# The input's own accumulate issued ahead of the base, operands begun in three slots of four, and the last block's first half in h's banks

## The chip, the cores and the metric

One core of a Trainium2 chip runs the whole program. The metric is device time in microseconds (us), the median of several executions. Engines are named as the profile names them: PE (TensorE), DVE (VectorE), ACT (ScalarE), POOL (GpSimd), SP (SyncE); PEld is PE's weight load.

## What is computed

2048 tokens of 512 features are normalised; the result is the input plus a state-space convolution of the normalised rows plus a mixture of eight experts, all eight of which every token uses:

```python
x = A_u
xn = _layernorm(x, axis=-1)
return x + _A_ref(xn, ...) + _B_ref(xn, ...)

# in _A_ref: K from dt, A, B, C (512 features, 128 states), then a causal convolution by FFT, and
y = ... + u * Dskip[None, None, :]

# in _B_ref, with K = E = 8, D = 512, F = 1792:
for e in range(E):
    mask = (topk_idx == e)
    w = (gates * mask).sum(-1, keepdims=True)
    h = _silu(xf @ w1[e]) @ w2[e]
    out = out + w * h
```

## The kernel before

**Blocks and slots.** The experts' work runs over 32 blocks: expert `e` (0 to 7) outside, quarter of the tokens `tb` (0 to 3, 512 tokens each) inside. A block runs over four steps `d` (three with two pairs of feature groups, the last with one), each step over four slots `s`. Seven products take the place of eight (Strassen's scheme), each in three fp16 parts. A step computes products of `w1` and `xop` into three PSUM banks, `hb`; ACT copies partial sums out of them (`scC`, `sE`, `scB`) or copies one bank into another (`hb<-hb`), and two DMAs that POOL issues add `sE` into `scC` (in slot 2) and into `scB` (in slot 3). ACT takes the summed `scC` up (L1584) at the start of the next step.

**The side of w2.** Before block (6,2), a unit is a product `y` of `ahl` and `w2s` (L1551 to L1553). From (6,2) on (`seven`), this side uses seven products too: `prep` brings a step's four quarters into operands `pl` and `st` in three stages (`prep_sums` on DVE, `prep_high` on ACT, `prep_low` on DVE), `pops2` gives PE units of 21 matmuls (L1783) on four banks `z`, once operands are ready, and `reads` takes a finished half (`th`, 1 ahead of 0) out of these banks. The last half of the last block uses the banks of `hb` and one more.

**What sums up the result.** `oacc[i]`, one DRAM tile for each 128 tokens, collects it. Expert 0 writes `ye` there (L1531), later experts add theirs by accumulating DMAs on POOL's queue (L1529); the four `ye` of a block are issued in the next block. In blocks (1,1), (1,2), (2,1) and (2,2), `base(i)` loads normalised rows, `base_add(i)` scales them by `Dskip` on DVE, and `base_send(i)` adds them into `oacc[i]` (L1512), then adds the input's rows `u` from DRAM (L1514). The convolution's result `ys4` is added at the end (L2010). For the first eight `i`, `oacc` is then copied to `out` (L2012); the last four are loaded back, combined in SBUF and sent in halves.

**What sets the order.** The program is written out in one order for each engine: `slot` calls the pieces of a slot in turn, `put(key, f)` hangs a piece on a slot, and a planner with estimated costs (`clock`, `room_now`) decides which conversions of weights go into a slot. Each engine issues its own instructions in that order, DMAs included, and a wait holds what is behind it on its queue. Two DMAs that accumulate into the same `oacc[i]` are kept apart by a wait of the issuing queue for the first one's landing.

Of the kernel before, what the change touches and what calls it, by code (L numbers as in the profile page):

```python
# [14 lines left out]
ALU = mybir.AluOpType  # L15
# [3 lines left out]
P = 128  # L19
# [17 lines left out]
def s4_moe_kernel(  # L37
# [15 lines left out]
    nc = tc.nc  # L53
# [3 lines left out]
    NT = NTOK // P  # L57
    KT = D // P
    E, NPR = w1.shape[0], w1.shape[1]
    NF = 2 * NPR  # L60
    TB = 512
    NB = NTOK // TB
    TPB = TB // P
# [8 lines left out]
    BG0 = (0, 2, 1, 0)  # L72
    SW = (6, 2)
    ROOM = 0.0
    LAG = 3

    RING = 2
# [27 lines left out]
    oacc = [dr.tile([P, D], F32, name=f"oacc{i}") for i in range(NT)]  # L105
# [387 lines left out]
    rows = {}  # L493
# [607 lines left out]
    def now():  # L1101
        return clock["slot"]
# [205 lines left out]
    for pr in range(3, NPR):  # L1308
        for h in range(2):
            n = 2 * (pr - 3) + h  # L1310
# [170 lines left out]
    def room_now():  # L1481
        return min(clock["actleft"], 2.0) + clock["pe"] - clock["pe1"] - clock["act"] + clock["act0"]
# [27 lines left out]

    def base_send(i):
        nc.gpsimd.dma_start(oacc[i], stg[i], accum_op=ALU.add)  # L1512
        halves = [a.rearrange("p (h d) -> h p d", h=2) for a in (oacc[i], u[i * P:(i + 1) * P, :])]
        nc.gpsimd.dma_start(*halves, accum_op=ALU.add)  # L1514


    units = []
# [94 lines left out]
    pipe = {"step1": None, "step2": None, "began": 0, "ended": 0, "popped": False, "out": [], 0: 0, 1: 0, "pool": 0}  # L1612
# [37 lines left out]
    def place():  # L1650
        if pipe["pool"] < RING:
            return "pool"
        if live["n"] > NRAW - 2 or any(h > m for h, m in zip(held_q, (10, 2, 2))) or any(it.load and it.raw is None and it.ready() for it in work[:6]):
            return None
        return "raw"
# [57 lines left out]
        for q, pr in enumerate(DQS[d]):  # L1713
            units2.append((k, q, pr, now()))

    def prep():


        for n in (2, 1):
            if pipe[f"step{n}"] and (n == 2 or place() and (ready2() == 0 or room_now() > 0.5)):  # L1720
                if n == 1:
                    reserve(pipe["step1"][0])
                x, pipe[f"step{n}"] = pipe[f"step{n}"], None
                (prep_high, prep_low)[n - 1](x)
                if n == 1:
                    pipe["step2"] = x
        if order and not pipe["step1"] and now() > pipe["began"] + (len(open_) > 1 and len(order) < 6):
            k = order[0]
            if all((*k, f) in quarters and quarters[(*k, f)][1] < now() for f in range(2)):
                order.pop(0)  # L1730
                pipe["began"] = now()
                pipe["step1"] = prep_sums(k)
# [5 lines left out]
    def ready2():  # L1738
        n = 0
        for k, q, pr, at in units2:  # L1740
            if at >= now() or not w2_made(k[0], pr):
                break
            n += 1
        return n
# [15 lines left out]
    def pop2():  # L1760
        (e, tb, th, d), q, pr, _ = units2.pop(0)
        key = (e, tb, th, 2)
        c = count.get(key, 0)
        last = e == E - 1 and tb == NB - 1
        todo = [(open_[e, tb, th, d], q, pr)]
        if last and th == 0 and d > 1:
            while units2:
                k, q1, pr1, _ = units2.pop(0)
                todo.append((open_[k], q1, pr1))
        count[key] = c + len(todo)  # L1770
        if c == 0 and last and th == 0:
            take_bank()
            ys[key] = [*hb, ps_s.tile([P, 2, TH], F32, tag="s4", name="z3")]
        elif c == 0:
            ys[key] = [ps_y.tile([P, 2, TH], F32, tag=f"y{n}", name=f"z{e}_{tb}_{th}_{n}") for n in range(4)]
        began = set()
        for b, h, fa, ia, fb, ib in SEQ:
            for m, ((pl, st), q1, pr1) in enumerate(todo):
                wx, ws = x2["w"][pr1], w2s[pr1].rearrange("p a f (h c) -> p a (f h) c", h=2)
                rhs = ws[:, :, (0, 2, 3)[ib], :] if not fb else wx[:, :, ib - 1, :] if ib else ws[:, :, 1, :]  # L1780
                for n, (x, y) in enumerate(((0, 0), (0, 1), (1, 0))):
                    lhs = st[:, x, ia, q1, :] if fa else pl[:, x, q1, ia, :]
                    T.matmul(ys[key][b][:, h], lhs, rhs[:, y, :], start=(c == 0 and b not in began and m + n == 0),  # L1783
                             stop=(count[key] == NPR and m + 1 == len(todo) and n == 2), skip_group_check=True)
                began.add(b)
        clock["pe"] += 2.3 * len(todo)
        if q == len(DQS[d]) - 1:
            del open_[e, tb, th, d]
            release((e, tb, th, d))
            if th == 0:  # L1790
                done.add((e, tb, "y", d))
        if count[key] == NPR:
            pipe["ended"] = now()
            pipe["out"].append(lambda: (read_last if last else read)(e, tb, th, ys.pop(key)))
# [47 lines left out]
    def reads():  # L1842
        if "send" in pipe and pipe["send"][0] < now():
            pipe.pop("send")[1]()
        while pipe["out"]:
            pipe["out"].pop(0)()
# [12 lines left out]
    def put(key, f):  # L1859
        side.setdefault(key, []).append(f)  # L1860
# [45 lines left out]
    for tb in range(NB):  # L1906
        for j in range(TPB):
            i = tb * TPB + j
            eb = (1 + tb // 2, 1 + tb % 2)
            for n, f in ((7, base), (8 + j % 2, base_add), (11, base_send)):  # L1910
                n += 3 if j > 1 else 0
                n += 1 if j > 1 and f is base_send else 0
                put((*eb, n // 4, n % 4), lambda i=i, f=f: f(i))
        if tb:
            put((0, tb, 2, 0), lambda tb=tb: gates_mm(tb))
            put((0, tb, 2, 1), lambda tb=tb: gates_dve(tb))
# [11 lines left out]
    halves = [(g, a) for g in (2, 3) for a in range(2)]  # L1928
# [34 lines left out]
    def slot(e, tb, d, s, pops):  # L1963
        if "s4" in done and not x2 and (True, (SW[0], "w2", NPR - 1)) in made:
            second_open()
        for key in [key for key in late if key in done]:
            work[0:0] = late.pop(key)
        for f in mid.get((e, tb, d, s), ()):
            f()
        clock["conv"] = clock["read"] = 0  # L1970
        if e + tb == 0:
            work_lows()
        if seven(e, tb):
            if units:
                pop(min((2, 2, 1, 0)[s], len(units)))
            else:
                pops2(s)
        else:
            pop(pops)
        flush()  # L1980
        if seven(e, tb):
            prep()
        if e == 0:
            work_lows()
        room = clock["room"] = act_room()
        if room > 1.0 and run_later():
            room = min(room - 1.6, 1.0 if s in (1, 2) else room)
        for f in side.get((e, tb, d, s), ()):
            f()
        work_lows()  # L1990
        if e + tb and (d, s) == (len(DQS) - 1, 1):
            held.append(room)
        elif e + tb == 0 or tb == NB - 1:
            work_on(2 if e + tb == 0 or room > 2 and (e or d < 3) else 1)
        elif e == 0 and tb == 1:
            work_on(2 if (d, s) < (2, 1) else 1 if (d, s) == (2, 1) else 0)
        elif seven(e, tb):
            work_on(2 if room > (1.0 if e > SW[0] else 2.2) else 1 if room > -1.0 else 0)
        elif room > 1.0:
            work_on(1 if room < 2.2 or 0 < e and not x2 else 2)  # L2000
        if (e, tb, d, s) >= BG0:
            if (e, tb, d, s) == BG0:
                clock["pe"] = clock["pe0"] = clock["pe1"] = clock["dve"] = clock["dve0"] = 0.0
            bg_run()
        if seven(e, tb):
            reads()
        clock["slot"] += 1

    def s4_final(i):
        nc.gpsimd.dma_start(oacc[i], ys4[:, i, :], accum_op=ALU.add)  # L2010
        if i < NT - 2 * TPB:
            nc.sync.dma_start(out[i * P:(i + 1) * P, :], oacc[i])  # L2012

    for i in range(NT):
        put((E - 1, NB - 1 - (i >= NT // 2), i // 2 % 4, i % 2 * 3), lambda i=i: s4_final(i))

    def final_load(j):
        i = NT - TPB + j
# [145 lines left out]
    while units2 or order or pipe["step1"] or pipe["step2"]:  # L2164
        if units2 and pipe["out"] and units2[0][0][1:3] == (NB - 1, 1):
            reads()
        if units2 and units2[0][0] == (E - 1, NB - 1, 0, 2) and len(units2) < 3:
            pass
        else:
            pops2(None)  # L2170
        prep()
        if not order and not pipe["step1"] and not pipe["step2"]:
            reads()
        clock["slot"] += 1
# [57 lines left out]
```

## Time and profile before

| | us |
|---|---|
| median of three executions | 2514.57 (2514.34 to 2518.81) |
| the profiled execution | 2521.78 |
| its span on the core | 2519.7 |
| PE busy | 2313.6 |
| DVE busy | 1933.0 |
| ACT busy | 1522.8 |
| POOL busy | 373.8 |

In the profile, busy tenths show the span in 40 slices of 63 us; PEclk is the granted TensorE clock in tenths. In a list of waits, a row says which engine and line waited for which, us in total, times, and the longest. In a timeline a row has the start, the time from the first start to the last end, the engine and line, the operation and its tiles, and in brackets the idle time ahead of it with what ended it. A DMA's row gives its count, its KB and the median us from issue to landing.

### The profile page before, as it was taken

To read this page: it belongs to the slowest core of one execution; us is meant where nothing else is said; L and a number is where in the kernel's file an instruction comes from. 1 tells how busy PE (TensorE), PEld (TensorE's weight loads), DVE (VectorE), ACT (ScalarE), POOL (GpSimd) and SP (SyncE) were. 2 spreads that over 40 slices of the span, in tenths; PEclk is the share of its full clock that TensorE was granted. 3 is DMA by queue.
4 is the path that set the end of the run, shared out by engine and by line. 5 is a ranking of instruction groups with operands and counts; after the bars stand their busy time and mean duration, and the time that the engine had idled before them with its cause. 6 is when DMAs were issued, how large, how long until landed. Compare 5 with 4: busy or idle time off the path is not lost.

```text
span 2519.7 us, 48492 instructions
## 1 busy us (share of the span) xinstructions
PE 2313.6 (92%) x19033; PEld 1631.9 (65%) x19033; DVE 1933.0 (77%) x3868; ACT 1522.8 (60%) x2665; POOL 373.8 (15%) x411
## 2 busy tenths in 40 slices
PE   8999999575999493999999999999999999999996
PEld 4666666353666362666666666666666668878885
DVE  8868998574998383998999999999878343875556
ACT  7676766252666252666667666766656766766553
POOL 0000001111111111111111011111101111111220
PEclk9999999887999797999999999999999999999998
DMA  7686656453657462665555565566545666543662
GB/s 264 207 242 156 158 133 139 89 120 68 141 141 156 72 136 40 144 146 124 125 102 135 147 131 124 102 147 146 121 99 134 174 148 147 133 114 72 110 109 60
DMA packets 366357, 331.00 MB, mean 131 GB/s; under 512 B 216304, under 2 KB 256880, under 8 KB 365680
## 3 DMA queue, kind: packets, MB, share of 16 engines
q1 hardware_dynamic: 276656, 229.35, 31.4%
q0 software_dynamic: 88896, 98.03, 25.3%
q8 instruction: 149, 2.44, 0.4%
q14 instruction: 80, 0.66, 0.1%
q10 hardware_dynamic: 576, 0.52, 0.1%
HBM read 211.97 MB, written 70.25 MB: 112 GB/s over the span
## 4 chain that ended last, share of the span: by engine, by line
PE 73%; issue 10%; DMA 9%; DVE 3%; ACT 3%; POOL 2%; SPq 0%; DVEq 0%; POOLq 0%; ACTq 0%
PE hb L1568 33%; PE y L1552 10%; PE y L1553 10%; PE y L1551 10%; PE z L1783 5%; DMA scC<-sE 4%; DMA oacc<-base 1%; DMA scB<-sE 1%; PE kgen L922 1%; PE yp L1072 1%; PE uf L985 1%; PE kf L985 1%; POOL oacc L1512 1%; PE hb L2124 1%; DVE ahl L1597 0%
## 5 line engine op out<-in xcount | busy, mean ns | idle before, releaser
L1568 PE MATMUL hb<-xop,w1s 128*128 128x256 f16 x9114 | 1087.6, 275 | 134.9 <-ACT hb L2079 115.3
L1568 PEld LDWEIGHTS <-w1s 128*128 128x128 f16 x9114 | 891.9, 99 | 304.4 <-issue 137.5
L1552 PE MATMUL y<-w2s,ahl 128*128 128x512 f16 x1456 | 551.8, 379 | 0.9 <-DVE w2s L566 0.9
L1553 PE MATMUL y<-w2s,ahl 128*128 128x512 f16 x1456 | 551.8, 379 | 0.0
L1551 PE MATMUL y<-w2s,ahl 128*128 128x512 f16 x1456 | 551.8, 379 | 0.0
L2026 POOL DMA_DIRECT2D scC<-sE x117 | 114.6, 979 | 1152.1 <-ACT sE L2064 962.6
L1553 PEld LDWEIGHTS <-ahl 128*128 128x128 f16 x1456 | 142.5, 98 | 172.8 <-issue 1.2
L1552 PEld LDWEIGHTS <-ahl 128*128 128x128 f16 x1456 | 142.5, 98 | 130.5 <-issue 0.2
L1551 PEld LDWEIGHTS <-ahl 128*128 128x128 f16 x1456 | 142.5, 98 | 130.4
L1597 DVE SCALAR_TENSOR_TENSOR ahl<-scC,sc,ahl 128x512 f16<-128x512 f32 x100 | 67.9, 679 | 195.8 <-ACT ahl L1588 195.8
L1584 ACT ACTIVATE scC<-scC,sc 128x512 f32<-128x512 f32 (+1 forms) x97 | 64.8, 668 | 215.8 <-DMA scC<-sE 215.7
L1584 ACT ACTIVATE fa<-hb,sc 128x512 f32<-128x512 f32 (+1 forms) x204 | 129.6, 635 | 107.0 <-PE hb L1568 105.2
L1597 DVE SCALAR_TENSOR_TENSOR ahl<-fa,sc,ahl 128x512 f16<-128x512 f32 (+1 forms) x214 | 146.0, 683 | 50.7 <-ACT ahl L1588 50.2
L2026 POOL DMA_DIRECT2D scB<-sE x124 | 118.4, 955 | 394.4 <-ACT scB L2064 275.3
L2079 ACT COPY hb<-hb 128x512 f32<-128x512 f32 x124 | 64.4, 520 | 176.1 <-PE hb L1568 175.9
L1588 ACT ACTIVATE ahl<-fa,sc 128x512 f16<-128x512 f32 (+1 forms) x214 | 143.7, 672 | 8.6 <-DMA xnd<-xn 1.4
L908 DVE TENSOR_TENSOR tb<-tb,pt 128x64 f32<-128x64 f32 (+2 forms) x192 | 132.3, 689 | 6.6
L906 DVE TENSOR_TENSOR pt<-tb,zi 128x64 f32<-128x64 f32 (+2 forms) x192 | 131.5, 685 | 4.8
L1040 DVE TENSOR_TENSOR s<-s,tm 128x672 f32<-128x672 f32 (+6 forms) x224 | 127.8, 570 | 7.7
L2069 ACT COPY hb<-hb 128x512 f32<-128x512 f32 x124 | 64.9, 524 | 110.3 <-PE hb L1568 109.8
L907 DVE TENSOR_TENSOR tb<-tb,zr 128x64 f32<-128x64 f32 (+2 forms) x192 | 130.6, 680 | 0.0
L1039 DVE TENSOR_TENSOR tm<-v,k 128x672 f32<-128x672 f32 (+6 forms) x224 | 126.7, 566 | 4.6
(332 smaller groups left out, 3391.5 us busy)
## 6 DMA issues: line engine op xcount, KB each, us to landing
xop<-xd SPq DMA_DIRECT2D x210, 256.0 KB, 4.1
pp<-in_w_dram SPq DMA_DIRECT2D x98, 512.0 KB, 4.7
raw<-in_w_dram SPq DMA_DIRECT2D x56, 512.0 KB, 4.8
scB<-sE POOLq DMA_DIRECT2D x93, 256.0 KB, 4.1
scC<-sE POOLq DMA_DIRECT2D x89, 256.0 KB, 4.0
oacc<-ye POOLq DMA_DIRECT2D x88, 256.0 KB, 6.4
raw<-in_w_dram SPq DMA_DIRECT2D x52, 256.0 KB, 3.8
raw<-in_w_dram SPq DMA_DIRECT2D x104, 128.0 KB, 3.9
```

What stands on the lines that cost most here:

```text
L906: V.tensor_tensor(pt, tin[:, ::-1, r], ziv, op=ALU.mult)
L907: V.tensor_tensor(tout[:, :, r], tin[:, :, r], zrv, op=ALU.mult)
L908: V.tensor_tensor(tout[:, :, r], tout[:, :, r], pt, op=ALU.add)
L1040: V.tensor_tensor(s3[:, :, m:], s3[:, :, m:], tm, op=ALU.add)
L1551: T.matmul(y, lhs[0], w2s[pr][:, 0, fh, :], start=(c == 0), stop=False)
L1552: T.matmul(y, lhs[0], w2s[pr][:, 1, fh, :], start=False, stop=False)
L1553: T.matmul(y, lhs[1], w2s[pr][:, 0, fh, :], start=False, stop=(c == NF - 1))
L1568: T.matmul(dst[:, q, :], w1s[pr][:, a, wo, k * P:(k + 1) * P], xop[:, xo, b, k, :], start=(first_mm and q == 0 and n == 0), stop=(n == 5), ...
L1584: S.activation(fa, src[:, :n], AF.Silu, scale=w1_unscale(e, d if whole else prs[0]))
L1588: S.activation(ahl[:, 0, :n], fa, AF.Copy, scale=scales[e][:, 3:4])
L1597: V.scalar_tensor_tensor(ahl[:, 1, :n], fa, sc[:, 3:4], ahl[:, 0, :n], op0=ALU.mult, op1=ALU.subtract)
L2026: nc.gpsimd.dma_start(dst, src, accum_op=ALU.add)
```

## The change

There are five parts.

1. `base_send` no longer adds the input. A new `base_u(i)` does: the DMA's form is two times 64 rows of 512 elements (even and odd rows) where it was two times 128 rows of 256 (left and right halves), and it is put in slots 1 and 3 of steps 0 and 1.
2. `prep` gets the slot and begins `prep_high` only in slots 0 to 2, and only if the planner's `room_now` is over `RUSH` (0.0), also where no unit is ready. `reads` is called once more in a slot, right behind `prep`.
3. In these blocks one conversion of weights is allowed where `room` is over `TIGHT` (-0.3), before: over -1.0.
4. In the last block the first half (`th` = 1) goes to the banks of `hb` and the further bank, and the second half (`th` = 0) to the four banks `y`; before it was the other way round.
5. The copy of `oacc` to `out` is put in a slot of its own (`final_out`).

```diff
+    RUSH = 0.0
+    TIGHT = -0.3
...
     def base_send(i):
         nc.gpsimd.dma_start(oacc[i], stg[i], accum_op=ALU.add)
-        halves = [a.rearrange("p (h d) -> h p d", h=2) for a in (oacc[i], u[i * P:(i + 1) * P, :])]
-        nc.gpsimd.dma_start(*halves, accum_op=ALU.add)
+
+    def base_u(i):
+        rows = [a.rearrange("(b a) d -> a b d", a=2) for a in (oacc[i], u[i * P:(i + 1) * P, :])]
+        nc.gpsimd.dma_start(*rows, accum_op=ALU.add)
...
-    def prep():
+    def prep(s):
         for n in (2, 1):
-            if pipe[f"step{n}"] and (n == 2 or place() and (ready2() == 0 or room_now() > 0.5)):
+            if pipe[f"step{n}"] and (n == 2 or place() and s < 3 and room_now() > (0.5 if ready2() else RUSH)):
...
-        if c == 0 and last and th == 0:
+        if c == 0 and last and th == 1:
             take_bank()
             ys[key] = [*hb, ps_s.tile([P, 2, TH], F32, tag="s4", name="z3")]
...
             eb = (1 + tb // 2, 1 + tb % 2)
+            put((*eb, j // 2, 1 + j % 2 * 2), lambda i=i: base_u(i))
             for n, f in ((7, base), (8 + j % 2, base_add), (11, base_send)):
...
         if seven(e, tb):
-            prep()
+            prep(s)
+            if pipe["out"]:
+                reads()
...
-            work_on(2 if room > (1.0 if e > SW[0] else 2.2) else 1 if room > -1.0 else 0)
+            work_on(2 if room > (1.0 if e > SW[0] else 2.2) else 1 if room > TIGHT else 0)
...
     def s4_final(i):
         nc.gpsimd.dma_start(oacc[i], ys4[:, i, :], accum_op=ALU.add)
-        if i < NT - 2 * TPB:
-            nc.sync.dma_start(out[i * P:(i + 1) * P, :], oacc[i])
+
+    def final_out(i):
+        nc.sync.dma_start(out[i * P:(i + 1) * P, :], oacc[i])
 
     for i in range(NT):
         put((E - 1, NB - 1 - (i >= NT // 2), i // 2 % 4, i % 2 * 3), lambda i=i: s4_final(i))
+        if i < NT - 2 * TPB:
+            put((E - 1, NB - 1, min(i // 2 + i % 2, 3), (3, 1)[i % 2] + (i == NT // 2 - 1) * 2), lambda i=i: final_out(i))
...
-        prep()
+        prep(0)
```

Line numbers of the changed kernel are 4 to 10 higher than those of before. How the order on the engines moves is shown at two places. Up to block (6,2) only POOL's order differs; SP's is the same from end to end.

**POOL, block (1,1).** A name like `scC1_1_2` gives e, tb and d; `in_u_dram` is the input. Before, from the last adds of step 2 on:

```order
L2026 DMA scB1_1_2_5541<-sE1_1_2_5474 128x512
L1512 DMA oacc0_109<-base0_5279 128x512
L1514 DMA oacc0_109<-in_u_dram 2x128x256
L1512 DMA oacc1_110<-base1_5281 128x512
L1514 DMA oacc1_110<-in_u_dram 2x128x256
L2026 DMA scC1_1_3_5695<-sE1_1_3_5704 128x256
L2026 DMA scB1_1_3_5739<-sE1_1_3_5704 128x256
L1512 DMA oacc2_111<-base2_5491 128x512
L1514 DMA oacc2_111<-in_u_dram 2x128x256
L1512 DMA oacc3_112<-base3_5493 128x512
L1514 DMA oacc3_112<-in_u_dram 2x128x256
L2026 DMA scC1_2_0_5913<-sE1_2_0_5927 128x512
```

The four adds of the input are gone from there in the changed kernel, and stand in the first half of the block:

```order
L1518 DMA oacc0_109<-in_u_dram 2x64x512
L2036 DMA scC1_1_0_4913<-sE1_1_0_4927 128x512
L2036 DMA scB1_1_0_5036<-sE1_1_0_4927 128x512
L1518 DMA oacc1_110<-in_u_dram 2x64x512
L1533 DMA oacc2_111<-ye1_2_5129 128x512
L1533 DMA oacc3_112<-ye1_3_5132 128x512
L1533 DMA oacc0_109<-ye1_0_5141 128x512
L1533 DMA oacc1_110<-ye1_1_5144 128x512
L1518 DMA oacc2_111<-in_u_dram 2x64x512
L2036 DMA scC1_1_1_5195<-sE1_1_1_5209 128x512
L2036 DMA scB1_1_1_5265<-sE1_1_1_5209 128x512
L1518 DMA oacc3_112<-in_u_dram 2x64x512
```

The input's adds moved ahead of the base, two of them to either side of the four `ye`, which in this block add into the same `oacc`; `scC` of step 1 now stands right behind the third.

**ACT, block (7,1), between steps 2 and 3.** `pl` and `st` are the operands that `prep_high` writes, `o` the reading of a finished half, `hb1<-hb0` the copy with which step 3 begins. Before:

```order
L2064 COPY scB7_1_2_27045<-hb1_103 128x512
L1697 ACTIVATE pl7_0_0_1_27069<-q7_0_1_0_26011,sc7_23973 128x2x128
L1697 ACTIVATE pl7_0_0_1_27069<-scB7_0_1_26121,sc7_23973 128x2x256
L1697 ACTIVATE st7_0_0_1_27070<-sums7_0_0_1_26981,sc7_23973 128x1024
L1797 COPY o7_2_0_27079<-z7_0_1_0_26469 128x256
L2069 COPY hb1_103<-hb0_102 128x256
L1646 ACTIVATE scC7_1_2_26999<-scC7_1_2_26999,sc7_23973 128x512
```

And in the changed kernel:

```order
L2074 COPY scB7_1_2_27045<-hb1_103 128x512
L1801 COPY o7_2_0_27069<-z7_0_1_0_26469 128x256
L2079 COPY hb1_103<-hb0_102 128x256
L1650 ACTIVATE scC7_1_2_26999<-scC7_1_2_26999,sc7_23973 128x512
L1701 ACTIVATE pl7_0_0_1_27087<-q7_0_1_0_26011,sc7_23973 128x2x128
L1701 ACTIVATE pl7_0_0_1_27087<-scB7_0_1_26121,sc7_23973 128x2x256
L1701 ACTIVATE st7_0_0_1_27088<-sums7_0_0_1_26981,sc7_23973 128x1024
```

The three operand instructions moved from ahead of the bank copy to behind it and behind the take-up of `scC`. On PE, units that came in pairs at the start of a half come one at a time, a slot later.

## The prediction

> **What bounds the kernel now.** I read the page first, its slices above all, then the busy time block by block, then the waits, then the timeline at the places they name. (A block is one expert, e, on one quarter of the tokens, tb; four steps d, each of four slots s.)
>
> ```profile
> span 2519.7 us, 48492 instructions
> PE 2313.6 (92%) x19033; PEld 1631.9 (65%) x19033; DVE 1933.0 (77%) x3868; ACT 1522.8 (60%) x2665; POOL 373.8 (15%) x411
> PE   8999999575999493999999999999999999999996
> PEclk9999999887999797999999999999999999999998
> ```
>
> TensorE is the bound nearly everywhere; it has two holes, slices 7 to 9 and 13 to 15, and a short last slice. The holes by blocks (the stretches run from one block's first scC add to the next one's; columns: us, then PE, PEld, DVE, ACT, POOL busy, granted clock, DMA share, GB/s):
>
> ```profile
> 312.60:384.90 72.30, 72.30 (x577) 48.78 (x576) 67.74 (x122) 45.28 (x79) 6.91 (x9) 1.00 0.51 126
> 384.90:496.30 111.40, 89.95 (x805) 60.71 (x804) 81.58 (x172) 53.35 (x104) 21.46 (x21) 0.91 0.55 114
> 496.30:607.90 111.60, 76.91 (x650) 51.76 (x649) 72.31 (x155) 45.38 (x87) 22.19 (x22) 0.86 0.54 104
> 607.90:685.20 77.30, 61.49 (x419) 40.40 (x417) 57.36 (x96) 45.59 (x73) 11.43 (x13) 0.89 0.56 124
> 685.20:758.90 73.70, 73.51 (x641) 49.66 (x640) 69.27 (x142) 49.18 (x87) 10.58 (x12) 1.00 0.60 137
> 758.90:869.30 110.40, 89.45 (x754) 60.54 (x753) 73.97 (x147) 51.23 (x98) 21.22 (x20) 0.91 0.56 114
> 869.30:984.80 115.50, 78.13 (x653) 52.55 (x651) 70.16 (x148) 44.27 (x83) 22.25 (x21) 0.84 0.51 99
> 984.80:1064.70 79.90, 60.55 (x414) 39.92 (x413) 58.63 (x103) 46.39 (x77) 11.47 (x14) 0.87 0.55 122
> 1064.70:1139.40 74.70, 72.88 (x629) 49.04 (x628) 70.68 (x142) 48.76 (x87) 10.41 (x12) 1.00 0.58 134
> ```
>
> A block without base work takes 72.3, 73.7, 74.7: 73.6 in the mean. The six stretches that the four base blocks touch sum to 606.1, so the holes cost 606.1 - 6 x 73.6 = 164.5 us, PE's slower clock there included. Who is waited for in them (us in total, times, longest; all but the first row from windows over the holes):
>
> ```profile
> POOL oacc L1514 <- DMA oacc<-base: 175.8, 14, 18.6
> ACT scC L1584 <- DMA scC<-sE: 96.0, 6, 27.4
> ACT scC L1584 <- DMA scC<-sE: 101.7, 5, 27.7
> PE hb L1568 <- ACT hb L2079: 91.3, 6, 21.0
> PE yp L206 <- ACT k L1003: 35.6, 2, 18.0
> ```
>
> ACT waits 197.7 us in the two holes for the add of sE into scC, which POOL issues, and TensorE then waits for ACT's copies behind it. On POOL in block (1,1):
>
> ```profile
> 367.93 0.86 POOL L2026 DMA_DIRECT2D scB<-sE  x1 [1.80 <-ACT scB L2064]
> 391.22 0.86 POOL L2026 DMA_DIRECT2D scB<-sE  x1 [5.50 <-ACT scB L2064]
> 401.00 3.54 POOL L1529 DMA_DIRECT2D oacc<-ye  x4 [8.93 <-ACT ye L1525]
> 404.19 1.25 POOL L2026 DMA_DIRECT2D scC<-sE  x1
> 408.83 0.86 POOL L2026 DMA_DIRECT2D scB<-sE  x1 [3.39 <-ACT scB L2064]
> 457.23 1.96 POOL L1514 DMA_DIRECT2D oacc<-in_u_dram  x1 [18.57 <-DMA oacc<-base]
> 458.33 1.83 POOL L2026 DMA_DIRECT2D scC<-sE  x1
> 473.29 0.51 ACT L1584 ACTIVATE scC<-scC,sc 128x256 f32<-128x256 f32 x1 [27.40 <-DMA scC<-sE]
> ```
>
> POOL holds its queue until base has landed, then issues u, then the scC that stood behind it; ACT has it 473.29 - 458.33 = 15.0 after its issue and 16.1 after u's. So an add queued just behind u arrives with u.
>
> ```profile
> scC<-sE POOLq DMA_DIRECT2D x89, 256.0 KB, 4.0
> oacc<-ye POOLq DMA_DIRECT2D x88, 256.0 KB, 6.4
> oacc<-in_u_dram POOLq DMA_DIRECT2D x16, 256.0 KB, 15.8
> DMA to landing us min/median/max: 15.0/15.8/19.6
> ```
>
> The same 256 KB take 4.0 and 6.4 from SBUF, 15.8 from u (last row: u's line alone).
>
> **The change, part by part.** *u ahead of base (POOL).* What goes: 14 waits of u on base, and u's from the stretch between scC of steps 2 and 3 and the next block's first scC. With them go both ACT waits of each base block: -164.5. What comes: the same 16 u's, issued elsewhere. POOL issues as soon as its queue allows, so u0 goes out at once behind scB of the block before (367.93), 17 us ahead of this block's first scC (384.9): hidden, just, at 15.8. u1 goes out behind scB of step 0, at 391.22 + 0.86 = 392.1, lands 407.9. In (1,1) and (1,2) the four ye's add into the very rows of these u's: the last waits for u1 (natural 401.0 to 404.5, now 407.9), and u2 waits for the first ye, so it issues near 409. scC of step 1 (naturally 404.19) is right behind it and is used 16.1 after u2's issue, at 425.1. When would ACT want it? In block (2,0), without u:
>
> ```profile
> 705.60 0.86 POOL L2026 DMA_DIRECT2D scC<-sE  x1 [0.67 <-ACT sE L2064]
> 714.93 0.72 ACT L1584 ACTIVATE scC<-scC,sc 128x512 f32<-128x512 f32 x1 [0.74 <-DMA scC<-sE]
> ```
>
> ACT is there 714.19 - 705.60 = 8.6 after the issue: 412.8. So ACT waits 12.3. In (2,1) and (2,2) the ye's are other rows' and nothing waits: u2 issues at 404.5, scC is used at 420.6 if u1 and u2 run beside each other (wait 7.8), or 12.3 again if they run one after the other; I take 10, the middle, as no row shows which. u3 follows scB of step 1 and has 15 us until the (now later) scC of step 2: hidden. Base goes out where it did, waits for nothing new, and lands with the 6.4 of its like. Sum of ACT waits 2 x 12.3 + 2 x 10 = 44.6, against 197.7 before, which cost 164.5: at 0.83 per us, 37.
>
> The size of u's transfer is the one unknown: 64 rows of 512 elements in each of two parts in place of 128 rows of 256. Bounds from the rows: 6.4 (ye, same bytes, same destination) and 19.6 (slowest u). At 6.4 no add is late; at 19.6 u1 lands 411.7, u2 issues near 413, scC is used at 433, ACT waits 20 x 4, which is 66. I take 15.8, since source, destination, bytes and the count of two parts stay. The Trainium skill ("DMA: Bandwidth & Descriptors", Rules for kernel authors) says that an outermost dim of c < 16 confines a DMA to at most c engines; by that the new form is still on two engines, and u is no shorter. The trace's 15.8 against 6.4 for equal bytes agrees. The page adds (Why a DMA increments its semaphore by 16 and not by 1) that such small counts go to the next engines in turn; by that u1 and u2 would run beside each other, and the wait in (2,1) and (2,2) would be 7.8, some 4 us less in all. No row here shows it.
>
> *Cover that goes.* The holes hid DVE work: 81.58 + 72.31 + 57.36 = 211 us of DVE in three stretches that shrink from 300 to some 240, 88% busy. Other blocks run at 67.74 of 72.30 without a hole, so I charge 4 us in all (0 to 12).
>
> *prep in three of four slots, reads earlier, the two thresholds* (blocks from (6,2) on). PE's waits from 2060 us to the end:
>
> ```profile
> PE hb L1568 <- ACT hb L2069: 8.1, 5, 1.8
> PE hb L1568 <- ACT scC L2064: 7.3, 5, 2.4
> PE z L1783 <- DVE o L1798: 4.3, 2, 2.9
> PE hb L1568 <- ACT hb L2079: 3.3, 1, 3.3
> ```
>
> The five waits of the first row stand where the order of ACT shows three prep operations ahead of the hb copy; now they stand behind it: -8.1. On DVE and PE nothing is added, units come one at a time and a slot later. New waits of like size can appear behind the moved prep (the copy at L2079 is next): +2. Net -6; bounds -19 (all ACT waits of these rows go) and +8 (each moved one costs as much elsewhere).
>
> *Last block's first half in h's banks.* One stall at the end goes, where that half had to wait until the half before was read out of the y banks:
>
> ```profile
> 2465.69 0.49 PE L1783 MATMUL z<-w2s,pl 128*128 128x256 f16 x3 [2.87 <-DVE o L1798]
> 2467.46 0.80 PE L1783 MATMUL z<-w2s,st 128*128 128x256 f16 x3 [0.63 <-DVE o L1811]
> 2469.97 0.85 PE L1783 MATMUL z<-w2s,pl 128*128 128x256 f16 x3
> 2494.61 1.32 ACT L1818 ACTIVATE o<-o,gse 128x512 f32<-128x512 f32 x2
> ```
>
> 2.87 + 0.63, and some 2 us of triples at 0.85 in place of 0.49; but DVE works on the same operands at that time, so I take -3 (0 to -6). The closing chain stays as it is: the gate of block (7,2)'s last half (L1818) is still issued behind the last prep, and the final loads behind that.
>
> *final_out apart.* SP's order is the same row for row: 0.
>
> Sum: -164.5 + 37 + 4 - 6 - 3 = -132.5. The profiled execution took 2521.78 (span 2519.7), the median of the runs is 2514.57, 0.3% less; on the median 2514.57 - 132.5 = 2382.
>
> **The rivals.**
> - *No wait remains* (u lands in 6.4, or runs beside everything): -164.5 - 9 + 4, 2345. For it: the rows are twice as long and half as many. Against: 15.8 for the same bytes and the same two parts.
> - *The queue stays full*: u's run one after the other, u0 also delays scC of step 0 and u3 that of step 2. It needs only some 3 us more on each; ACT would wait some 25 to 30 in each base block, 83 to 100 us of cost in place of 37: 2430 to 2445. For it: the longest u took 19.6, and four u's of 15.8 are 63 of a block's 73.6 us.
> - *Slower than before*: u's form of longer rows costs more per byte. If they run one after the other, a base block can't be shorter than four of them: from 18.4 us a piece on the queue never empties and every add waits. The gain of 170 is used up where 4 u - 73.6 = 42, at 29 us for one u; at 32 us the blocks lose 4 x (128 - 73.6) = 218, and the time is 2514.57 - 164.5 + 218 + 4 - 9 = 2563. Nothing in the rows points to a price near that.
> - *The change doesn't do what it says*: u's new waits (ye on u, u on ye) hold POOL as base did. They exist in (1,1) and (1,2) alone, and are in the sum.
>
> **How the numbers follow.** A change under 0.2% (5 us) can't be told from none here. Chances: my forecast 0.62 (2355 to 2425), no wait 0.15, full queue 0.17, slower 0.04, within 0.2% 0.02. The forecast's range goes down to 2350 and up to 2430, which leaves out most of the first rival and of the second: 0.94 faster, 0.02 same, 0.04 slower.
>
> **What would show it.** The wait of POOL's u on base is gone; POOL waits some 4 us for u1 ahead of a ye in (1,1) and (1,2). ACT's waits for scC<-sE in the two stretches sum to about 45, all at step 1, 8 to 12 each; at steps 3 and 0 none is left. The base blocks take about 83 in place of 111, with the granted clock near 1. u lands in 14 to 17. The five waits on ACT hb at what is now L2079 are gone from (7,0) on, and at the last half's start PE waits under 1 us. Wrong would be: waits for scC at steps 0 or 2 (full queue), u under 10 or over 20, or a DVE that is over 95% busy in the base blocks with PE waiting for it.

## The result, and the profile after

The changed kernel takes 2402.24 us (median of 4 runs, 2398.95 to 2405.74) against 2516.14 for the kernel before on the same chip: a ratio of 0.9547, 95% interval 0.9529 to 0.9564. It is faster by 114 us. Forecast were 132.5 us less and 2382, range 2350 to 2430. The profiled execution took 2403.11 us with a span of 2401.3, so the trace shows 118.4 us less span than the one of before.

The head and the slices of its page, against those quoted of before:

```profile
span 2401.3 us, 48485 instructions
PE 2306.6 (96%) x19033; PEld 1627.8 (68%) x19033; DVE 1931.0 (80%) x3868; ACT 1523.4 (63%) x2665; POOL 365.2 (15%) x411
PE   8999999789998899999999999999999999999996
PEclk9999999899999999999999999999999999999998
```

The holes at slices 7 to 9 and 13 to 15 (counted from 0) have become two shallow dips of sevens and eights (slices 7 and 8, 12 and 13), and PE's share went from 92 to 96%. The same by blocks (columns as before: us, then PE, PEld, DVE, ACT, POOL busy, granted clock, DMA share, GB/s):

```profile
384.90:475.10 90.20, 75.48 (x642) 51.02 (x641) 67.62 (x146) 47.85 (x93) 20.05 (x20) 0.92 0.67 139
475.10:565.40 90.30, 78.26 (x666) 52.54 (x665) 76.37 (x157) 46.23 (x89) 18.65 (x19) 0.94 0.65 128
565.40:636.90 71.50, 71.50 (x564) 48.12 (x563) 67.31 (x124) 50.08 (x83) 10.45 (x12) 1.00 0.58 135
711.00:794.10 83.10, 74.61 (x590) 50.27 (x589) 63.16 (x128) 45.97 (x87) 20.05 (x21) 0.96 0.74 160
794.10:879.70 85.60, 77.10 (x666) 52.15 (x665) 66.33 (x139) 46.57 (x90) 18.60 (x19) 0.94 0.66 135
879.70:953.20 73.50, 71.70 (x564) 48.03 (x563) 71.47 (x132) 49.62 (x83) 10.58 (x12) 1.00 0.55 131
```

The six stretches sum to 494.2 in place of 606.1: 111.9 less. The third and the sixth are now plain blocks (71.5 and 73.5; 73.6 is the mean of the plain ones), so nothing is left over from one block to the next. The four base blocks themselves still cost 494.2 - 441.6 = 52.6 us; 41 were forecast.

Who waits there, over all base blocks (380 to 960 us):

```profile
ACT scC L1588 <- DMA scC<-sE: 57.1, 6, 18.1
DVE base L1510 <- DMA base<-xnd: 42.7, 4, 16.8
```

POOL's wait of u on base (175.8 us) is gone. ACT's waits for scC fell from 197.7 to 57.1, not to 44.6. Four of them make 56.4, one behind u2 in each base block: 18.1 in (1,1) and 12.3 in (1,2), where 12.3 was forecast for each, and 14.0 in (2,1) and 12.1 in (2,2), where 10 was. The second row, VectorE's wait for base's loads (15.0 us before), was in no term of the sum. POOL and ACT in block (1,1), from the timeline, some rows between left out:

```profile
391.84 1.71 POOL L1518 DMA_DIRECT2D oacc<-in_u_dram  x1
409.95 0.86 POOL L1533 DMA_DIRECT2D oacc<-ye  x1 [6.19 <-ACT pp L559]
412.48 1.43 POOL L1518 DMA_DIRECT2D oacc<-in_u_dram  x1 [1.67 <-DVE ahl L1601]
413.32 1.56 POOL L2036 DMA_DIRECT2D scC<-sE  x1
414.42 2.79 POOL L1518 DMA_DIRECT2D oacc<-in_u_dram  x1
430.58 0.72 ACT L1588 ACTIVATE scC<-scC,sc 128x512 f32<-128x512 f32 x1 [18.06 <-DMA scC<-sE]
```

This is the chain of the forecast, link by link: u1 goes out at 391.84 (392.1 forecast), the fourth ye waits for it (the row names another releaser, but u1 landed at 409.45, 0.5 ahead of the ye), u2 goes out behind the ye, scC right behind u2, and ACT has scC 18.1 after u2's issue. Each link is a little late, and they add up: u1 lands 1.5 later than forecast, u2 goes out 3.5 later, scC is used 5.5 later. The landing behind it, from u's line alone:

```profile
DMA to landing us min/median/max: 14.3/17.7/21.2
```

### The profile page after: what moved, and what is told of

Read it like the earlier page. It is cut to its first block, busy times and chain, and to the rows that moved or that the text cites. A ratio compares the mean times of both kernels' runs of the same rounds, so it can differ in the third digit from the quotient of the medians.

```text
span 2401.3 us, 48485 instructions
## 1 busy us (share of the span) xinstructions
PE 2306.6 (96%) x19033; PEld 1627.8 (68%) x19033; DVE 1931.0 (80%) x3868; ACT 1523.4 (63%) x2665; POOL 365.2 (15%) x411
## 3 DMA queue, kind: packets, MB, share of 16 engines
q0 software_dynamic: 72512, 97.92, 26.1%
## 4 chain that ended last, share of the span: by engine, by line
PE 80%; DMA 7%; DVE 5%; issue 5%; ACT 3%; POOL 0%; SPq 0%; DVEq 0%; ACTq 0%; POOLq 0%
PE hb L1572 37%; PE y L1556 11%; PE y L1557 11%; PE y L1555 11%; PE z L1787 6%; DMA scC<-sE 3%; PE kgen L924 1%; PE kf L987 1%; PE yp L1074 1%; DMA ys<-ysb 1%; PE uf L987 1%; DVE ahl L1601 1%; PE hb L2134 1%; DVE tm L1041 0%; PE tp L338 0%
## 5 line engine op out<-in xcount | busy, mean ns | idle before, releaser
L2036 POOL DMA_DIRECT2D scB<-sE x124 | 110.3, 890 | 422.8 <-ACT scB L2074 306.1
L2079 ACT COPY hb<-hb 128x512 f32<-128x512 f32 x124 | 64.8, 523 | 128.1 <-PE hb L1572 127.5
```

What stands on the lines that cost most here:

```text
L2036: nc.gpsimd.dma_start(dst, src, accum_op=ALU.add)
```

## The experiments

Each run stood beside runs of the kernel before on its chip (medians of 2516.1 to 2519.1); the ratio is to those. "Six stretches" is the sum over the same six stretches as above, from each run's own trace.

| run | median us | ratio (95%) | six stretches |
|---|---|---|---|
| before | 2516.14 | 1 | 606.1 |
| the change | 2402.24 | 0.9547 (0.9529 to 0.9564) | 494.2 |
| e2 u's part alone | 2410.81 | 0.9573 (0.9560 to 0.9586) | 493.7 |
| e3 the rest alone | 2513.87 | 0.9985 (0.9976 to 0.9994) | 605.7 |
| e4 halves at the new place | 2406.92 | 0.9564 (0.9549 to 0.9579) | 499.6 |
| e9 last half undone | 2405.86 | 0.9547 (0.9532 to 0.9561) | 496.0 |
| e1 16 parts | 2361.12 | 0.9384 (0.9371 to 0.9397) | 452.2 |
| e11 4 parts | 2371.98 | 0.9419 (0.9403 to 0.9435) | 461.8 |
| e6 16 parts at the old place, nothing else | 2360.39 | 0.9373 (0.9359 to 0.9387) | 447.7 |
| e12 16 parts at the old place, the rest kept | 2356.89 | 0.9357 (0.9340 to 0.9373) | 445.8 |
| e5 no u | 2352.61 | 0.9338 (0.9325 to 0.9350) | 444.2 |
| e7 base later | 2408.20 | 0.9564 (0.9547 to 0.9581) | 502.7 |
| e8 u2 and u3 later | 2406.16 | 0.9545 (0.9526 to 0.9565) | 497.0 |
| e10 16 parts and base later | 2353.34 | 0.9342 (0.9330 to 0.9355) | 446.5 |

**Which part of the change did it.** e2 is the kernel before with base_u and its place alone; e3 is the changed kernel with u put back behind each base add in its old form, so the prep, the reads, the thresholds, the last half and final_out alone.

> The kernel before with part 1 alone: the input's add in rows form, at the new places. Theory (the gain lies in the base blocks): the stretches of the base blocks as in the changed kernel (90, 90, 71.5, 83, 86, 73.5), the blocks from (6,2) on as before: 2402 + 8 = 2410, 2406 to 2414. Rival (parts 2 to 5 carry much of the gain, or the parts help each other): 2420 or more.

> The changed kernel without part 1: the input's add in halves behind the base again, parts 2 to 5 kept. Theory: 8 us under the kernel before (5.3 in the blocks from (6,2) to (7,2), 2.5 behind the last block's begin): 2506 to 2510, ratio 0.9955 to 0.998. Rival (those parts are worth nothing measurable, the two traces' difference there is chance): ratio 0.999 to 1.001.

u's part is worth 4.3%, as expected. The rest is worth 0.15%, 2 to 6 us by its interval: less than the traces had led me to expect (0.9985 lies above the theory's range and just below the rival's), but its interval leaves out 1. The form was changed with the place, so e4 puts the old form (two halves of 128 rows by 256) at the new place:

```
-        rows = [a.rearrange("(b a) d -> a b d", a=2) ...
+        rows = [a.rearrange("p (h d) -> h p d", h=2) ...
```

> The changed kernel with the input's add at its new places but in the old form, two parts of 128 rows of 256. Theory (time on the queue goes by bytes per part, not by rows): landing 15 to 19 us, time within 5 us of the changed kernel's 2402. Rival (longer rows shorten the transfer, part of the gain is the form's): landing over 20 us in the base blocks, 2412 to 2430.

As expected: u in halves lands in 19.0 (median) in place of 17.7, and the intervals of the two ratios overlap. With two parts, rows half as long and twice as many make little difference. e9 undoes the choice for the last block's halves:

```
-        if c == 0 and last and th == 1:
+        if c == 0 and last and th == 0:
```

> The changed kernel with one choice undone: the last block's first half in the y banks again, and its second in h's, as before. By the two traces (from the last block's first scC to the end 119.4 us before, 116.9 after) it costs 2 to 4 us: 2404 to 2407, ratio 0.9555 to 0.957, with a wait of PE's z for o of 2 to 3 us at the last half's start again. Rival (nothing but noise of the schedule): 2400 to 2403, ratio 0.954 to 0.955.

The time can't tell it: the medians differ by 3.6 us, as expected, but the ratios of the two series are both 0.9547, which is in the rival's range. The trace does: from the last block's first scC to the end it takes 2403.6 - 2284.2 = 119.4 again (before 119.4, after 2401.3 - 2284.4 = 116.9), and the wait is back at the last half's start (2 to 3 us were expected). The longest of TensorE's waits from there on in e9:

```profile
PE z L1787 <- DVE o L1802: 3.8, 1, 3.8
```

**What u's length is worth.** e1 leaves the change as it is and cuts u into 16 parts of 8 rows in place of 2 of 64; e11 into 4 of 32:

```
-        rows = [a.rearrange("(b a) d -> a b d", a=2) ...
+        rows = [a.rearrange("(b a) d -> a b d", a=16) ...   # e11: a=4
```

> The changed kernel with the input's add written as sixteen parts of 8 rows of 512 elements in place of two parts of 64; places unchanged. Theory (the add's long stay on the queue, 17.7 us to landing, is what the scC of step 1 and the ye's wait for): landing falls to that of the ye's, 5 to 8 us, ACT's waits for scC<-sE in the base blocks fall from 57 us to under 10, and the four base blocks take 73 to 75 us each; 2402 less the 52.7 us that the six stretches still cost, 2350 to 2358. Rival (the count of parts is indifferent, what is left comes from the order of POOL's queue and DVE's load): 2395 to 2405, landing 14 or more.

> The changed kernel with u in 4 parts of 32 rows by 512 elements, in place of 2 parts of 64. u landed in 17.7 us (median) with 2 parts and in 8.1 with 16. Theory (each part's rows are carried by one engine, one after the other, so that the time falls with the number of parts): a part's rows take half as long as with 2, u lands in 11 to 14 us, ACT waits 15 to 30 us for scC in the base blocks, time 2364 to 2380 (ratio 0.939 to 0.946). Rival (the gain of 16 parts comes only with all 16 engines): u lands in over 15, time over 2390.

e11 is as its theory said (ACT's waits for scC 29.9 us). e1 goes the theory's way and falls a little short of it: 3 us above its range, with 14.5 us of ACT's waits for scC where under 10 were expected. u's landing with 4 parts, and then with 16:

```profile
DMA to landing us min/median/max: 8.8/11.8/16.7
```

```profile
DMA to landing us min/median/max: 5.2/8.1/12.4
```

17.7, 11.8 and 8.1 us for the same bytes at the same places, and the time follows: 2402, 2372, 2361. The rows kept their length; fewer rows in a part alone did little at two parts (e4: 19.0 with 128, the change: 17.7 with 64), so the number of parts is what counts. The waits of e1 over the base blocks:

```profile
DVE base L1510 <- DMA base<-xnd: 20.6, 4, 7.4
ACT scC L1588 <- DMA scC<-sE: 14.5, 5, 4.6
```

Both fell, though only u was touched: VectorE's wait, too, hung for the most part on u (without any u, in e5 below, it is 10.5). Part of the path from u to base's loads is seen on SP's own queue: the loads wait for a buffer that a ye gives back when it has landed, and the ye's land behind u. In (2,1) u1 lands at 737.4, the first two ye's at 738.9 and 740.2, and SP issues the first two loads at 738.9 and 740.2. SP's waits of this kind over the base blocks, in the changed kernel and in e1:

```profile
SPq L1505 <- DMA oacc<-ye: 15.3, 4, 7.1
SPq L1505 <- DMA oacc<-ye: 2.2, 2, 1.3
```

**Is the new place needed at all?** e6 is the kernel before with one line edited, u in 16 parts behind each base add where it always was. e12 is the changed kernel with the same, so that the rest of the change is in both e12 and e1.

> The kernel before with one edit: u stays where it was, each behind its base add, but goes out as 16 parts of 8 rows by 512 elements. Theory (u's long transfer is the cause of all three waits: u's own landing, the base add that stands behind an earlier u, and scC behind both): base lands in 6 to 8 us in place of 18, u in 8 in place of 16, so scC of steps 3 and 0 comes about 20 us sooner of the 27 that ACT waited; ACT's waits fall from 198 to 50 to 80 us and the time to 2390 to 2420 (ratio 0.950 to 0.962), about what the new place alone gave (2411). Rival (the order is the cause: u waits for base's landing whatever the size): two landings one after the other remain in each place, ACT still waits 15 us each time, time 2440 to 2470 (ratio 0.97 to 0.98).

> The changed kernel with u in 16 parts and back at its old place, behind each base add; the other parts of the change stay. Against it stand u in 16 parts at the new place (2361.1, ratio 0.9384) and u in 16 parts at the old place without the other parts (2360.4, ratio 0.9373). Theory (with a short u the place is worth nothing, and the other parts are worth about 4 us): 2353 to 2358, ratio 0.9345 to 0.9370. Rival (the new place is worth something still, and the two runs differ by chance): 2362 to 2368, ratio 0.938 to 0.941.

My expectation of e6 missed by 30 us on the good side: the shape alone, at the old place, is as fast as shape and place together. Its slices, then POOL in block (1,1), first in the kernel before and then in e6:

```profile
PE   8999999999999999999999999999999999989996
```

```profile
430.06 1.22 POOL L1512 DMA_DIRECT2D oacc<-base  x1
435.74 1.96 POOL L1514 DMA_DIRECT2D oacc<-in_u_dram  x1 [4.46 <-DMA oacc<-base]
436.85 1.81 POOL L1512 DMA_DIRECT2D oacc<-base  x1
457.23 1.96 POOL L1514 DMA_DIRECT2D oacc<-in_u_dram  x1 [18.57 <-DMA oacc<-base]
```

```profile
430.02 1.22 POOL L1512 DMA_DIRECT2D oacc<-base  x1
436.05 0.89 POOL L1514 DMA_DIRECT2D oacc<-in_u_dram  x1 [4.81 <-DMA oacc<-base]
436.62 1.27 POOL L1512 DMA_DIRECT2D oacc<-base  x1
445.05 0.88 POOL L1514 DMA_DIRECT2D oacc<-in_u_dram  x1 [7.16 <-DVE ahl L1597]
445.60 1.26 POOL L2026 DMA_DIRECT2D scC<-sE  x1
```

The waits that the change took away are still there, and they are short: POOL waits ahead of each of the 16 u's, 87.2 us in all where it was 203.8, whatever releaser the rows name. Over the base blocks in e6 the profile names base for nine of them:

```profile
POOL oacc L1514 <- DMA oacc<-base: 47.1, 9, 7.8
ACT scC L1584 <- DMA scC<-sE: 23.9, 11, 5.4
```

Why they are short is in base's landing; its line in the kernel before, then in e6:

```profile
DMA to landing us min/median/max: 4.8/15.7/19.8
```

```profile
DMA to landing us min/median/max: 5.0/5.9/8.9
```

Before, a base add took 15.7 us where the same add at the same place takes 5.9 in e6: it stood behind the u before it. The trace of before held this already. The first base add of each block, with no u of the block ahead of it, landed in 4.8 to 5.8 us; the other twelve, each behind a u, took 15.3 to 19.8. So the wait "of u on base", 175.8 us, was for the most part the wait for the previous u. e12 against e1: 0.9357 and 0.9384, intervals that overlap a little, with the old place ahead. The new order of the adds shows no gain once u is short.

e5 takes u out altogether:

```
-            put((*eb, j // 2, 1 + j % 2 * 2), lambda i=i: base_u(i))
```

> The changed kernel with the sixteen adds of u left out (the result lacks the input). It is the floor for any form and place of them. In the changed kernel the six stretches around the base blocks still cost 52.7 us over six plain ones, and u in 16 parts took 40 of those. Theory (what is left there is u's transfer and what stands behind it): 2345 to 2356 us, ratio 0.932 to 0.936, no wait of ACT for scC over 3 us in the base blocks, stretches of 73 to 75. Rival (the base adds and their loads cost as much by themselves): 2358 to 2366, no better than u in 16 parts at 2361.

2352.6, in the theory's range, with no wait of ACT's for scC over 2.9 us, though one stretch, (1,2)'s, still takes 79.1. This kernel leaves out the input, so it serves as the floor for anything done to u. e12 is 4 us above it, the change 50.

**What holds the changed kernel where it is.** Two rows stand in its base blocks, ACT's for scC and VectorE's for base. e7 takes the second away, e8 most of the first:

```
 e7:
-                n += 3 if j > 1 else 0
-                n += 1 if j > 1 and f is base_send else 0
+                n += 3
+                n += 1 if f is base_send else 0
 e8:
-            put((*eb, j // 2, 1 + j % 2 * 2), lambda i=i: base_u(i))
+            put((*eb, *((0, 1), (0, 3), (1, 3), (2, 3))[j]), lambda i=i: base_u(i))
```

> The changed kernel with the loads of base for the first two rows of a block three slots later (as those of the last two already were), their adds on VectorE with them, and every base add into the result one slot later still. That takes away VectorE's four waits for base's loads (42.7 us, longest 16.8). Theory (scC behind u on POOL's queue binds, VectorE's wait runs beside it): 2396 to 2405, ratio 0.952 to 0.956, ACT's waits for scC still 50 to 60 us in the base blocks. Rival (VectorE's wait is a path of its own and carries a good part of the remaining 53 us): 2375 to 2392, ratio 0.944 to 0.950.

> The changed kernel with u in its 2 long parts, but with the last two of a block's four u's in later slots: behind scB of step 1 and behind scB of step 2, in place of ahead of scC of step 1 and behind scB of step 1. Theory (scC of step 1 is late only since it stands right behind a u, and a long u is hidden in a place with a whole step ahead of the next scC): ACT's waits for scC in the base blocks fall from 57 to under 20 us, time 2360 to 2380 (ratio 0.938 to 0.946). Rival (four u's of 18 us leave no place in a block of 74; the wait moves to scC of step 2 or 3 and to base): 2388 to 2410 (ratio 0.949 to 0.957).

e7 left ACT's waits where its theory said and came out 3 us above its range; e8's theory fell, its time lies in the rival's range. Their rows over the base blocks, e7's and then e8's:

```profile
ACT scC L1588 <- DMA scC<-sE: 56.5, 5, 15.0
ACT ksb L933 <- DMA ys<-ysb: 15.6, 1, 15.6
DVE base L1510 <- DMA base<-xnd: 8.4, 5, 3.3
```

```profile
DVE base L1510 <- DMA base<-xnd: 49.8, 4, 14.6
ACT scC L1588 <- DMA scC<-sE: 15.9, 5, 7.0
ACT ksb L933 <- DMA ys<-ysb: 15.3, 1, 15.3
```

Each took its wait away, and neither gained: the other wait stood, and a third grew from 5.8 us in the changed kernel to over 15, ACT's for ys, which SP loads. e8 shows where it comes from, in block (1,2), on SP, POOL and ACT:

```profile
525.82 4.78 SPq L1086 DMA_DIRECT2D ys<-ysb  x4
526.07 1.88 POOL L1518 DMA_DIRECT2D oacc<-in_u_dram  x1
543.00 0.38 ACT L933 ACTIVATE ksb<-kgen 128x256 f32<-128x256 f32 x1 [15.35 <-DMA ys<-ysb]
```

The four loads go out between 525.8 and 529.7, u at 526.07 among them. The two loads issued before or just beside u land after 6.5 and 6.2 us, the next two after 12.2 and 13.2 (532.3, 532.7, 539.3, 542.9 in the trace), and u itself at 542.7. That u is the cause is shown at another place, which several runs share: near 369 us SP issues four loads of ys, and in the changed kernel u0 goes out there too, at 368.6. Their landing before (no u there), in the change (2 parts), in e1 (16 parts) and in e5 (no u):

```profile
DMA to landing us min/median/max: 2.1/2.6/3.5
DMA to landing us min/median/max: 9.6/12.0/12.7
DMA to landing us min/median/max: 4.1/4.3/4.5
DMA to landing us min/median/max: 2.1/2.2/2.9
```

So a long u makes late what is issued beside it, on SP's queue as well as on POOL's, and the places tried only chose whom it hits. Whether e7 and e8 together would have freed the long form was not tried.

e10 is e1 and e7 together:

> Both edits at once: u in 16 parts, and base three slots later. With u in 16 parts the base blocks still cost 12.5 us over plain ones, with 14.5 us of ACT's waits for scC and 20.6 us of VectorE's waits for base's loads. Theory: where scC no longer binds, VectorE's wait does, so that the later base is worth 3 to 8 us here: 2352 to 2359, ratio 0.935 to 0.9375. Rival (the later base adds crowd into step 3, ahead of scC of the next block's step 0): 2361 to 2370, ratio 0.938 to 0.942.

2353.3, as the theory said: with u short, the later base is worth 0.4% (0.9384 to 0.9342, intervals apart), where with u long (e7) it was worth nothing. It has the lowest median of the complete kernels here (its interval overlaps e12's), 49 us below the change and level with e5.

## Why the prediction was right, and where it was off

- *u ahead of base: -164.5, and +37 for scC.* Right in kind and place. POOL's wait on base is gone, no wait of ACT's over 0.5 us is left at steps 3 and 0, and the new waits are in (1,1) and (1,2): POOL waits 6.2 and 3.7 us ahead of a ye that goes out 0.5 after u1 has landed, and 1.7 and 0.5 ahead of u2. One wait was not forecast: in (2,1) u3 goes out only once u1 has landed, 2.4 us late; the trace does not show why. The mis-sized term is the +37. "I take 15.8, since source, destination, bytes and the count of two parts stay": the count did decide, as e4 and e11 show, but u landed in 17.7 at its new place, and the links of the chain gave ACT 57.1 us of waits in place of 44.6. At the forecast's price of 0.83 that is 10 us.
- *The wait that was missed.* "Who is waited for" was read for what the old place held, and VectorE's wait for base's loads was 15.0 us there. Ye's that land later hold SP's loads of base, and VectorE's queue stands behind them: 42.7 us. e7 shows that taking it away alone gains nothing. The base blocks together cost 12 us more than forecast (52.6 against 41, which is the 37 and the 4 for lost cover).
- *"At 6.4 no add is late."* Nearly so: with u at 8.1 (e1) ACT still waits 14.5 us for scC, and the time is 16 above that rival's 2345; without u it is 8 above. Its condition, a u that lands in some 6 us, was almost one number away from the change (16 parts in place of 2).
- *Parallel u's.* I took the middle, as no row showed which. In (1,1) u2 and u3 went out 1.9 us apart and landed 3.0 apart (429.3 and 432.3), so they ran beside each other. That agrees with what the Trainium skill says ("DMA: Bandwidth & Descriptors", Why a DMA increments its semaphore by 16 and not by 1: small counts go to the next engines in turn). Where the question was put, for u1 and u2 in (2,1) and (2,2), it stays open: u2 went out 7.8 and 3.5 us before u1 landed and took 21.2 and 20.2 us, and ACT's 14.0 and 12.1 are nearer to the price of one after the other (12.3) than to that of side by side (7.8).
- *Full queue, slower.* Neither came: 56.4 of the 57.1 us stayed at step 1, and nothing was handed on to the next block.
- *prep, reads, thresholds: -6.* From (6,2)'s first scC to the last block's it takes 313.1 in place of 318.4: -5.3. There the five waits on hb (now L2079) fell from 8.1 to 2.9 us in place of going altogether, and those on ACT scC from 7.3 to 3.1. *Last half: -3.* 116.9 in place of 119.4: -2.5, and e9 brings just that back. *final_out: 0.* Nothing was seen of it. e3 times the three together at -2 to -6, where -9 was forecast; with the 12 us of the base blocks, this is most of the 19 us between 132.5 and the 114 measured.
- *What would show it.* The base blocks were to take about 83 with a clock near 1: they took 90.2, 90.3, 83.1 and 85.6 with 0.92 to 0.96. PE was to wait under 1 us at the last half's start. The wait on o is gone, but three waits of hb on the last half's own operands, 1.32, 0.26 and 1.36 us, stand there now. The prediction had spoken of this as VectorE working on the same operands.

The sum held, but the diagnosis under it was half of the matter: the holes were laid to the order (POOL waits for base, then u, then scC), and the row that spoke for the length, 15.8 beside 6.4 for equal bytes, was used only to price the new place. The Trainium skill's rule that the prediction cited (an outermost dim of c < 16 confines a DMA to at most c engines) agrees with 17.7, 11.8 and 8.1 us at 2, 4 and 16 parts. By it the cure was one line, the rearrange of e6, worth 159 us alone (2519.1 to 2360.4 on the same chip), where the new place in the long form alone is worth 108 (2518.6 to 2410.8). That the change lands in its range is no proof of the diagnosis: moving a long transfer and shortening it remove the same holes.

## What to carry to other kernels

When a transfer takes 15.8 us and others of the same bytes take 4.0 and 6.4, ask first why it is long, and only then where to put it; a wait for X behind it may be a wait for it. A long transfer that is moved can make its new neighbours late, on other queues too (the loads of ys, 2.6 to 12.0 us); when taking one wait away gains nothing, see what else the same transfer holds. And if two waits stand side by side, neither removal alone says what the pair costs.

## What the runs showed of the hardware

The packets of POOL's queue count more than the rows sent. The queue's line (packets, MB, share) in before, the change, e11, e6 and e5, which has no u:

```profile
q0 software_dynamic: 88896, 98.03, 25.3%
```

```profile
q0 software_dynamic: 72512, 97.92, 26.1%
```

```profile
q0 software_dynamic: 64320, 97.85, 26.3%
```

```profile
q0 software_dynamic: 58176, 97.81, 26.3%
```

```profile
q0 software_dynamic: 55872, 93.61, 25.2%
```

Over e5, one u of the 16 adds 2,064 packets with 128 rows in a part, 1,040 with 64, 528 with 32 and 144 with 8; that is 16 times one more than the rows of one part each time, while the bytes hardly move. So the count goes by the rows of one part, whatever the number of parts: with 16 parts of 8 rows it is near the 128 rows sent, with 2 parts it is some 8 times the rows sent (1,040 for 128), with the old two halves 2,064 for 256. Halving the packets at two parts (e4 has 128 rows in a part and 88,896 packets, the change 72,512) moved the landing only from 19.0 to 17.7, so the packets alone do not make u long. And the same 16 parts land in 8.1 at the new place (e1) and in 4.9 at the old one (e12); what else is in flight at the two places was not separated. u's line in e12:

```profile
DMA to landing us min/median/max: 4.1/4.9/7.7
```
